# One wait fewer for GpSimd ahead of the cast loads of queries, values and keys

## The chip, the cores and the metric

The kernel runs on one core of one Trainium2 chip. The metric is the device time of one execution in microseconds. The kernel before takes 425.17 us (median of four runs, 424.15 to 426.18).

## The reference

Eight batches of eight heads, with 1152 positions of 64 numbers each, go through attention with pooled queries; the result goes through a feed-forward network without a nonlinearity.

```python
q_pool = q.reshape(B, H, S // 2, 2, D).mean(axis=3)      # 576 queries
scores = scale * q_pool @ k^T                            # 576 x 1152 per head
attn   = softmax(scores)
x      = (attn @ v) as [B*576, 8*64]                     # 4608 x 512
h      = (x @ w1) * (x @ w2) @ w3
out    = h @ w_out                                       # 4608 x 512
```

All inputs and the output are float32 in DRAM. w1 and w2 are 512 x 1024, w3 is 1024 x 1024, w_out is 1024 x 512.

## The kernel before

**Tiling.** Two heads make a pair; there are 32 pairs, four to a batch. For a pair the scores are computed transposed (keys on partitions), key block by key block, and cut into chunks of 512 columns per head. A chunk is computed on TensorE (`scores`, L254), goes through exp on ScalarE (`expo`, L264) into a ring in SBUF, and is multiplied with the values and a column of constants on TensorE (`attend`, L279); VectorE divides by the sums (`normalize`, L292 and L296). The results of two pairs are turned by three DMA transposes on SP's queue into xT (L304, L307), the feed-forward network's input.

**Feed-forward.** The product of w3 and w_out is made once (T). Each unit of 512 tokens then takes the groups pa and pb (x times w1 and w2, L372), gT (their product, on VectorE) and pp (gT times T, L390). An output tile of 128 tokens is written by VectorE in two halves from pp into `osb`, of which there are three buffers (L402), and stored by two DMAs on SP's queue (L411). These groups are fitted in between the attention's work on TensorE; what is left after the attention makes the tail.

**Order.** The order of every engine is written out by hand: one loop over `it`, with three chunks an iteration, and a table (PVS) of how many value products each iteration issues. Each engine runs its own instructions in order, and so does each DMA-issuing queue: SP's and GpSimd's (POOL's) are the two that matter here. The semaphore waits between engines follow from the tiles that are written and read.

**Preparation of queries and keys.** Inputs are loaded by POOL with DMAs that cast to fp16 on the way: `load_q` (L80), `load_k` (L88), `load_v` (L95). For the first eight pairs queries and keys are brought into shape on VectorE and TensorE. From pair 8 on, two pairs at a time go through `prep_dma`: POOL adds neighbouring queries (L121, `pool_q`), POOL copies the keys of each pair into order (L141), and SP issues one DMA transpose of both pairs' keys into kT (L144) and one of both pairs' queries into qT (L147). The loop calls it about two pairs ahead of the scores that need them:

```python
        elif prepped < NP and at >= prepped - 1.95:
            prep_dma(prepped)
            if loaded < NP:
                settled(prepped)
                load_two(loaded)
                loaded += 2
            prepped += 2
```

`settled` lets POOL copy one number out of the kT and one out of the qT just issued (L152), so that POOL stands until the transposes have landed. `load_two` then issues six DMAs on POOL's queue, two each for queries, values and keys of the next two pairs. POOL's next instructions are the additions and copies of that next `prep_dma`, which wait for these loads. This goes round eleven times with loads, for pairs 8 to 28; the last call, for pairs 30 and 31, has none behind it. Of the tiles concerned, kst and vst have four buffers (one a pair), qst, kT, qT and qp two (one for two pairs), kc one.

Of the kernel before, what the change touches and what calls it, by code (L numbers as in the profile page):

```python
# [8 lines left out]
FP16 = mybir.dt.float16  # L9
# [14 lines left out]
def kernel(  # L24
# [11 lines left out]
    nc = tc.nc  # L36
# [12 lines left out]
    const = ctx.enter_context(tc.tile_pool(name="const", bufs=1))  # L49
# [12 lines left out]
    vts = [const.tile([128, 2, NJ, VW], FP16, name=f"vt{i}") for i in range(4)]  # L62

    ident = const.tile([128, 128], FP16)
    seen = const.tile([1, 2], FP16)

    ctx.enter_context(tc.manual_schedule())

# [4 lines left out]
    kst, vst, qst, kT, qT, kTs, qTs, qps = {}, {}, {}, {}, {}, {}, {}, {}  # L73
# [74 lines left out]
            out=qTs[P // 2], in_=qps[P // 2].rearrange("p c u d -> p (c u d)"))  # L148

    def settled(P):  # L150
        for n, t in enumerate((kT[P], qT[P])):
            nc.gpsimd.tensor_copy(out=seen[:, n:n + 1], in_=t[0:1, 0, 0:1])  # L152

    kcs, kc2 = {}, {}

# [207 lines left out]
    def ffn_groups(t):  # L363
# [71 lines left out]
        out=ident, in_=ident, compare_op=ALU.not_equal, fill=1.0,  # L435
# [54 lines left out]
    for c in range(NF):  # L490
        t = (6, 7, 8, 9, 11, 12, 14, 15)[c]
# [14 lines left out]
    for it in range(NIT):  # L506
# [30 lines left out]
        if prepped < NPE:  # L537
            if it >= first_it(prepped) - (1 if prepped < 4 else 2):
                queue[0:0] = prep_groups(prepped)
                prepped += 1  # L540
                urgent = True
# [7 lines that stand above are left out]
# [3 lines left out]
        n = PVS[it]  # L552
# [54 lines left out]
```

## Time and profile before

| what | value |
|---|---|
| median of the runs | 425.17 us |
| profiled execution, own time | 426.18 us |
| its span, first to last instruction | 424.4 us |
| TensorE matmul (PE) busy | 405.2 us, 95% |
| ScalarE (ACT) busy | 326.3 us, 77% |
| VectorE (DVE) busy | 196.5 us, 46% |
| GpSimd (POOL) busy | 123.0 us, 29% |
| granted TensorE clock | 1.0 in all slices |
| loads of q, v, k: issue to landing, median | 5.9, 9.1, 10.7 us |
| kT and qT transposes: issue to landing, median | 4.7, 3.8 us |

The profile comes from the execution of 426.18 us. Its span is 1.8 us shorter than that time, which also has what lies before the first and after the last instruction. A busy TensorE is not a TensorE at its peak: matmuls are pipelined and their ends are modelled. In the table of waits each line says which engine's instruction waited for what, the total in us, how often, and the longest wait. In the chain and in the timelines the first number is the start in us from the beginning of the span and the second is the duration in us; the bracket at the end is the idle time of the engine before it and what ended it. SPq is SyncE's queue, which only issues DMAs. DMA share is the mean busy share of the core's 16 DMA engines; it can pass 1 where packets of several queues overlap on one engine.

### The profile page before, as it was taken

The numbers are of one execution on the slowest core, as the hardware profiler recorded it, in microseconds if no ns is written. First come the engines' busy times: TensorE is split into PE (matmuls) and PEld (weight loads), VectorE is DVE, ScalarE is ACT, GpSimd is POOL, SyncE is SP. The second block draws the span as 40 slices with busy tenths as digits, with TensorE's granted clock in tenths as the row PEclk, the third lists the DMA queues.
The fourth block names the chain that finished last, engine by engine and source line by source line (L and its number), as shares of the span: only waits on it lengthen the run. The fifth ranks groups of instructions, "written<-read, shape, count | busy, mean of one in ns | idle before, by whom it ended". The sixth has DMA issues, their size and how long they took to land.

```text
span 424.4 us, 12581 instructions
## 1 busy us (share of the span) xinstructions
PE 405.2 (95%) x5432; PEld 269.1 (63%) x5432; DVE 196.5 (46%) x406; ACT 326.3 (77%) x355; POOL 123.0 (29%) x171
## 2 busy tenths in 40 slices
PE   3998999999999999999999998999999999999995
PEld 1676777666686577565765685666765876544443
DVE  1446556454544553554454543554445444614130
ACT  4899899989888888988888897887788889133332
POOL 8334321343434215151615243433334000000000
PEclk9999999999999999999999999999999999999999
DMA  8999999598989979698989798988989750050404
GB/s 130 203 208 195 186 192 185 102 167 133 149 144 180 170 112 198 135 188 120 169 149 166 126 146 163 176 146 131 200 151 181 111 117 17 14 116 0 101 0 100
DMA packets 94728, 59.15 MB, mean 139 GB/s; under 512 B 65360, under 2 KB 85072, under 8 KB 94672
## 3 DMA queue, kind: packets, MB, share of 16 engines
q0 software_dynamic: 26544, 33.56, 49.6%
q1 hardware_dynamic: 67968, 24.66, 32.0%
q8 instruction: 42, 0.69, 0.6%
q10 hardware_dynamic: 160, 0.13, 0.1%
q14 instruction: 14, 0.11, 0.1%
HBM read 67.11 MB, written 9.44 MB: 180 GB/s over the span
## 4 chain that ended last, share of the span: by engine, by line
PE 38%; DMA 36%; POOL 10%; SPq 6%; ACT 5%; issue 3%; DVE 1%; POOLq 0%; ACTq 0%; DVEq 0%
DMA kst<-in_k_dram 24%; DMA qT<-qp 8%; PE psc L254 7%; PE po L279 7%; PE pa L372 7%; PE pb L372 7%; PE pp L390 6%; SPq L144 6%; ACT er L264 5%; PE pT L356 3%; POOL vst L95 3%; POOL qst L80 3%; DMA out_dram<-osb 2%; POOL kc L141 2%; POOL kst L88 1%
## 5 line engine op out<-in xcount | busy, mean ns | idle before, releaser
L264 ACT ACTIVATE er<-psc 128x1024 f16<-128x1024 f32 x324 | 307.7, 1025 | 47.1 <-PE psc L254 46.9
L279 PEld LDWEIGHTS <-er 128*128 128x128 f16 x2880 | 104.3, 98 | 23.2 <-issue 6.5
L279 PE MATMUL po<-vt,er 128*128 128x65 f16 x2880 | 111.6, 194 | 0.4 <-DVE xn L296 0.4
L254 PE MATMUL psc<-qT,kT 64*128 64x512 f16 (+7 forms) x1152 | 97.6, 290 | 7.7 <-ACT er L264 3.3
L384 DVE TENSOR_TENSOR gT<-pb,asb 128x512 f16<-128x512 f32 x72 | 49.8, 692 | 55.8 <-PE pb L372 55.1
L372 PE MATMUL pa<-xT,w1sb 128*128 128x512 f16 x288 | 74.2, 380 | 0.0
L372 PE MATMUL pb<-xT,w2sb 128*128 128x512 f16 x288 | 74.1, 380 | 0.0
L390 PE MATMUL pp<-T,gT 128*128 128x256 f16 (+1 forms) x488 | 67.9, 292 | 0.0
L254 PEld LDWEIGHTS <-kT 64*128 64x128 f16 x1152 | 46.5, 95 | 33.3 <-issue 13.5
L382 DVE COPY asb<-pa 128x512 f32<-128x512 f32 x56 | 38.7, 692 | 40.4 <-PE pa L372 39.2
L390 PEld LDWEIGHTS <-gT 128*128 128x128 f16 x488 | 45.6, 98 | 18.5 <-issue 3.7
L372 PEld LDWEIGHTS <-w2sb 128*128 128x128 f16 x288 | 26.4, 98 | 32.7 <-issue 3.9
L372 PEld LDWEIGHTS <-w1sb 128*128 128x128 f16 x288 | 25.1, 98 | 30.1 <-issue 6.2
L121 POOL TENSOR_TENSOR qp<-qst 128x1152 f16<-128x1152 f16 x12 | 28.3, 2357 | 45.5 <-DMA qst<-in_q_dram 45.5
L402 DVE TENSOR_SCALAR osb<-pp 128x256 f32<-128x256 f32 x49 | 20.7, 425 | 41.4 <-PE pp L390 29.7
L292 DVE RECIPROCAL rz<-po 128x5 f32<-128x5 f32 x64 | 12.4, 194 | 49.8 <-PE po L279 49.3
L296 DVE TENSOR_TENSOR xn<-po,rz 128x320 f16<-128x320 f32 x64 | 31.5, 492 | 2.2
L141 POOL COPY kc<-kst 128x576 int32<-128x576 int32 x24 | 16.2, 678 | 45.4 <-DMA kst<-in_k_dram 45.4
L88 POOL DMA_DIRECT2D kst<-in_k_dram x33 | 23.8, 723 | 9.4 <-DMA kst<-in_k_dram 3.8
L95 POOL DMA_DIRECT2D vst<-in_v_dram x32 | 23.2, 727 | 10.6 <-DVE vt L134 5.5
L399 ACT ACTIVATE osb<-pp 128x512 f32<-128x512 f32 (+1 forms) x12 | 7.0, 579 | 24.2 <-PE pp L390 24.2
L80 POOL DMA_DIRECT2D qst<-in_q_dram x32 | 19.9, 622 | 12.0 <-issue 2.7
(40 smaller groups left out, 129.0 us busy)
## 6 DMA issues: line engine op xcount, KB each, us to landing
qst<-in_q_dram POOLq DMA_DIRECT2D x32, 288.0 KB, 5.9
vst<-in_v_dram POOLq DMA_DIRECT2D x32, 288.0 KB, 9.1
out_dram<-osb SPq DMA_DIRECT2D x70, 128.0 KB, 2.4
kst<-in_k_dram POOLq DMA_DIRECT2D x31, 288.0 KB, 10.7
w3h<-in_moe_w_dram POOLq DMA_DIRECT2D x4, 512.0 KB, 14.9
xT<-in_moe_w_out_dram POOLq DMA_DIRECT2D x2, 512.0 KB, 13.9
w1sb<-in_moe_w_dram POOLq DMA_DIRECT2D x2, 512.0 KB, 16.4
w2sb<-in_moe_w_dram POOLq DMA_DIRECT2D x2, 512.0 KB, 17.5
```

The source lines that it names most:

```text
L80: nc.gpsimd.dma_start(out=qst[P // 2][o:o + 64].rearrange("p u t d -> p u (t d)"), in_=q[b, h0:h0 + 2].rearrange("u (p t) d -> p u (t d)", ...
L88: nc.gpsimd.dma_start(out=kst[P][:, :, js[0]:js[1], :], in_=k[b, h0:h0 + 2].rearrange("u (p j) d -> p u j d", j=NJ)[:, :, js[0]:js[1], :])
L95: nc.gpsimd.dma_start(out=vst[P].rearrange("p u j d -> p u (j d)"), in_=v[b, h0:h0 + 2].rearrange("u (p j) d -> p u (j d)", j=NJ))
L121: eng.tensor_tensor(out=qps[pp][r].rearrange("p c u d -> p u c d"), in0=src[:, :, :, 0, :], in1=src[:, :, :, 1, :], op=ALU.add)
L254: nc.tensor.matmul(t[:, u, o:o + ln].rearrange("p (c f) -> p c f", f=64), kT[P][s, j, :], qT[P][s, f0 // 64:(f0 + ln) // 64], start=True, ...
L264: nc.scalar.activation(out=er[:, :, r:r + CH], in_=psc.pop(c), func=AF.Exp, bias=0.0, scale=SCALE)
L279: nc.tensor.matmul(po[P, u][:, VW * x:VW * x + D + 1], er[:, u, r:r + 128], vts[P % 4][:, u, j, 0:D + 1], start=(m == 0), stop=(m == 44), ...
L296: nc.vector.tensor_tensor(out=xn[:, P % 2, :, u, :], in0=acc[:, :, 0:D], in1=rz.to_broadcast([128, 5, D]), op=ALU.mult)
L372: nc.tensor.matmul(p, w[:, mc, ft * 128:ft * 128 + 128], xT[:, mc, t0:t0 + 512], start=(mc == 0), stop=(mc == NC - 1))
L382: nc.vector.tensor_copy(out=asb[ft], in_=p)
L384: nc.vector.tensor_mul(out=gT[:, ft, :], in0=p, in1=asb.pop(ft))
L390: nc.tensor.matmul(p[:, 0:n], gT[:, ft, 128 * i:128 * i + 128], T16[:, ft, n * s:n * s + n], start=(ft == 0), stop=(ft == NF - 1))
```

## The change

`settled` keeps the copy out of kT and drops the copy out of qT; the tile that receives the number shrinks to one element. POOL then issues the six loads after the key transposes have landed, whatever the query transposes do.

```diff
-    seen = const.tile([1, 2], FP16)
+    seen = const.tile([1, 1], FP16)
...
     def settled(P):
-        for n, t in enumerate((kT[P], qT[P])):
-            nc.gpsimd.tensor_copy(out=seen[:, n:n + 1], in_=t[0:1, 0, 0:1])
+        nc.gpsimd.tensor_copy(out=seen, in_=kT[P][0:1, 0, 0:1])
```

## The prediction

> **What bounds the kernel now.** I read the page first (engine rows and the chain that ended last), then the chain in order of time, the table of waits between 80 and 345 us, and the places where TensorE itself stood still.
>
> ```profile
> span 424.4 us, 12581 instructions
> PE 405.2 (95%) x5432; PEld 269.1 (63%) x5432; DVE 196.5 (46%) x406; ACT 326.3 (77%) x355; POOL 123.0 (29%) x171
> PE 38%; DMA 36%; POOL 10%; SPq 6%; ACT 5%; issue 3%; DVE 1%; POOLq 0%; ACTq 0%; DVEq 0%
> ```
>
> TensorE is busy for 95% of the span, yet the chain puts 52% on DMA, POOL and SP. The chain in order of time shows why: from 82 to 294 us it runs round a loop that no compute engine paces. One turn of it:
>
> ```profile
> 270.15 1.24 POOL qst L80 x2
> 271.39 1.43 POOL vst L95 x2
> 273.52 11.85 DMA kst<-in_k_dram
> 286.12 2.70 SPq L144
> 288.86 4.42 DMA qT<-qp
> 294.07 0.89 PE pp L390 x8
> ```
>
> POOL issues six cast loads; the last keys land after 11.85 us; POOL copies them (L141), SP issues the key and the query transposes (L144, L147), and the two copies of line 152 hold POOL until both have landed. Then the next six loads are issued. Turns start at 103.93, 125.89, 150.23 ... 330.26 us by the issues of L144, 22.6 us each on average ((330.26 - 103.93) / 10). TensorE needs two pairs in about the same time: its first score matmuls of pairs 10 and 30 are at 112.8 and 340.3 us, 22.7 us per two pairs. So two things run at almost the same pace, and the question is what the slower one costs the other. The waits answer it:
>
> ```profile
> POOL seen L152 <- DMA kT<-kc: 61.0, 11, 6.6
> POOL seen L152 <- DMA qT<-qp: 11.2, 11, 1.7
> DVE osb L402 <- DMA out_dram<-osb: 4.5, 3, 2.4
> PE psc L254 <- DVE osb L402: 1.9, 2, 1.6
> PE psc L254 <- DMA qT<-qp: 1.2, 2, 0.7
> ```
>
> POOL waits long, but POOL is not the bound. TensorE loses 1.2 us to query transposes (two waits) and 1.9 us to output evictions that wait for an old store (two waits). That 3.1 us is nearly all of its idle time between 80 and 345 us. The places:
>
> ```profile
> 293.32 0.34 PE L254 MATMUL psc<-qT,kT 64*128 64x384 f16 x2 [0.70 <-DMA qT<-qp]
> 257.15 0.40 PE L254 MATMUL psc<-qT,kT 64*128 64x320 f16 x4 [1.64 <-DVE osb L402]
> ```
>
> **The change, part by part.** (1) *The wait and its copy go.* Eleven times POOL no longer waits for qT (11.2 us in all) nor runs the second copy (11 x 0.18 us): 13.2 us, or 1.2 us a turn. One turn, in POOL's timeline:
>
> ```profile
> 268.35 0.18 POOL L152 COPY seen<-kT 1x1 f16<-1x1 f16 x1 [4.83 <-DMA kT<-kc]
> ...
> 269.69 0.18 POOL L152 COPY seen<-qT 1x1 f16<-1x1 f16 x1 [1.16 <-DMA qT<-qp]
> 270.15 1.24 POOL L80 DMA_DIRECT2D qst<-in_q_dram  x2 [0.28 <-issue]
> ```
>
> The first load is issued 0.46 us after the copy that it follows, so it would be issued at 268.81 instead of 270.15.
>
> (2) *What moves.* All six DMAs (two q, two v, two k) move earlier on POOL's queue by that 1.2 us, past the landing of the query transposes and towards what SP issues behind these: the xT transposes (L304, L307) and the output stores (L411). Nothing is reordered on SP. Their buffers are no brake: POOL's loads show no wait for a buffer after 80 us.
>
> Does it hurt the query transposes, which TensorE waits for? Loads and transposes share the 16 DMA engines. The three stretches around the loads of 249.08 us (columns after the engines: granted clock, DMA share, GB/s):
>
> ```profile
> 248.60:249.60 1.00, 1.00 (x14) 0.60 (x14) 0.30 (x1) 0.69 (x2) 0.83 (x2) 1.00 0.38 84
> 249.60:250.30 0.70, 0.70 (x9) 0.63 (x7) 0.00 (x0) 0.70 (x2) 0.70 (x2) 1.00 0.12 22
> 250.30:251.30 1.00, 1.00 (x17) 0.91 (x15) 0.44 (x2) 1.00 (x2) 1.00 (x3) 1.00 0.94 58
> ```
>
> The DMA engines are nearly empty for 1.2 us after the issue: a load moves its first bytes some 1.2 us late. So in the new order the first bytes move about 0.6 + 1.2 = 1.8 us after kT has landed, while qT lands 0.8 to 1.9 us after kT in these eleven turns. The rule that speaks against the change is in the Trainium skill, "DMA: Bandwidth & Descriptors", section "Queues, rings and completion order": each DMA engine goes round-robin, packet by packet, between the queues that have work. By it, a query transpose that met the loads would run at half its pace. By the row the overlap is at most 0.1 us in one turn, so the price on qT is 0.1 us by the rule and nothing by the row; I take nothing. The same rule does bear on what follows qT. In the turns where four or six stores follow (L411 at 267.74, for one), the DMA share is 0.94 between 269 and 272 us: no gap is there to fill, and loads started earlier only share. In the turns where xT transposes follow, the share falls to 0.12 as above, and the 0.9 us saved there is real. So a turn gains between 0 (all shared) and 1.2 us (nothing shared); I take 0.7, nearer the row with the gap, since a load that shares still gets its half.
>
> (3) *What that is worth.* Before pair 18 five turns have been shortened, before pair 26 nine: leads of 5 x 0.7 = 3.5 and 9 x 0.7 = 6.3 us, against waits of 0.49 and 0.70 us. Both go: **-1.2 us**. Less than 0.15 us a turn would do. The lead can grow: the key transposes of pair 18 were issued at 195.2, and the scores that free their buffer ended at 179.0; such a margin is 12 to 16 us in all turns.
>
> (4) *The stores.* SP is in order, and before every turn it stands up to 12 us at L144 waiting for the key copy; stores and xT transposes queue behind. The first output tile of one unit was written at 247.66 but its store was issued at 249.54, behind L307, and landed at 256.55, 6.4 to 7.0 us later because the loads run then (2.4 us when they don't: 269.61 to 272.04). TensorE stood 1.64 us for its buffer. The next unit: written 291.70, issued 295.11, landed 302.62, stall 0.27. With leads of 5 and 6 us SP reaches these stores before they are written: 1.9 and 3.4 us earlier, more than either stall: -1.9 us. Against it: the store of 204.44 (landed 211.42, awaited by DVE for 0.77 us with no stall on TensorE) will fall into the middle of the loads rather than their start, where stores took 6.5 to 7.5 us instead of 5.8 to 6.5; and TensorE comes 0.5 us sooner. I price that at +0.7 us (bounds: 0, if the cover of about 0.8 us at the other stall is there too, and +1.9, if nothing is won on stores at all).
>
> Sum: -1.2 - 1.9 + 0.7 = **-2.4 us**. The profiled execution took 426.18 us (span 424.4 and 1.8 around it); it would take 423.8. It stands 1.0 us above the median of the runs shown, so from 425.17 the forecast is **422.8 us**, 0.6% faster. Everything after 345 us is TensorE's own work and only moves.
>
> **The rivals.** *A, the forecast*, 422.8, own range 421.5 to 423.9; chance 0.50. *B, only the query waits go*: stores find other loads to collide with and their 1.9 us remain: 425.2 - 1.2 = 424.0; chance 0.20. For it: stores and loads are not synchronised, and the lead only shifts where they meet. Against: both stalls had a store held up behind SP's wait for the keys. *C, the change does not shorten the turn*: the loop is limited by DMA work, not by its gaps; the keys then land when they did, and the time stays at 425.2; chance 0.12. For it: DMA shares of 0.88 to 1.01 in all turns. Against: a DMA share of 0.04 from 262.6 to 264.4 us, between the last key load and the first transpose, and the 0.12 above: the engines do idle in every turn. *D, slower: the first store of a unit lands too late.* Its place is the ring of three osb buffers: the fourth tile of a unit needs the first one's. In the unit of 247.66 TensorE would not have stood had the store landed 7.3 us after the tile was written (8.9 - 1.6); the unit of 204.18 took 7.2 without a stall, that of 291.70 took 10.9 with 0.27 us of it. So two units are tight. With loads on top of more stores (the longest store of this profile took 8.3 us from its issue) these two stand for the excess over 7.3 us each. It decides against the change when it costs 1.3 us more than all that is won, (1.2 + 1.9 + 1.3) / 2 + 7.3 = 9.5 us from written to landed; at the 10.9 us of the third unit it is 2 x 3.6 - 3.1 = +4.1 us: 429.3; chance 0.18.
>
> **How the numbers follow.** A measurement of this kernel tells about 0.3% (1.3 us) from no change. A is faster throughout (0.50); of B a quarter comes out just beyond 1.3 us (0.05), the rest is the same (0.15); C is the same (0.12); D is slower (0.18). Faster 0.55, same 0.27, slower 0.18. The range takes in A, B and C and the light end of D: 421.3 to 426.2 leaves out about 0.15 above and 0.05 below.
>
> **What would show it.** Right: eleven seen copies, first load issued 0.5 us after each; issues of L144 creep ahead, so that qT lands more and more before the scores of its pair (0.04 us before at pairs 18 and 26 now); no wait of TensorE on qT; stores of first tiles issued at once. Wrong: query transposes taking over 5 us from issue (they meet the loads after all); turns still 22.6 us long; or longer DVE waits on out_dram with TensorE standing behind them, above all in several units.

## The result, and the profile after

The changed kernel takes 424.58 us (median of 43 executions, 421.73 to 433.73) against 425.04 us (64 executions, 422.60 to 430.46): ratio 0.9972, 95% interval 0.9954 to 0.9990, so 0.28% faster. The ratio leaves out executions far above the fastest of their own kernel, among them the nine of the changed kernel beyond 428 us, which is why it stands below the ratio of the two medians. The mean of all executions has hardly moved: 425.30 us against 425.38. A repetition gave 0.9985 (0.9960 to 1.0010), an interval that reaches no change.

By that ratio the gain is half of the forecast, but it is no uniform half. 13 of the 43 executions took at most 422.6 us, where one of 64 did before; 9 took more than 428, where 6 of 64 did (in the repetition 3 of 22, against 2 of 68). The fastest quarter of the executions took at most 422.4 us, where before it took at most 424.3. So the change makes good executions about 2 us faster and, as it seems, adds bad ones.

The profile was taken of an execution of 426.08 us (span 424.3), 1.5 us above the median and as long as the one profiled before (426.18). Page of the changed kernel; its lines behind `settled` have numbers lower by one:

```profile
span 424.3 us, 12560 instructions
PE 404.5 (95%) x5432; PEld 268.2 (63%) x5432; DVE 197.4 (47%) x406; ACT 326.2 (77%) x355; POOL 121.0 (29%) x160
DMA 54%; PE 32%; POOL 6%; issue 3%; ACT 3%; SPq 1%; DVE 1%; POOLq 0%; DVEq 0%
```

The chain still runs round the loop of loads and transposes. Its waits, 80 to 345 us:

```profile
POOL seen L151 <- DMA kT<-kc: 58.1, 11, 6.6
...
DVE osb L401 <- DMA out_dram<-osb: 3.5, 2, 1.8
...
PE psc L253 <- DMA qT<-qp: 1.9, 3, 1.1
PE psc L253 <- DVE osb L401: 1.4, 2, 0.9
```

POOL's wait for qT is gone. TensorE still waits: 1.9 us for qT (1.2 before) and 1.4 us behind old stores (1.9 before), 3.3 us against 3.1. That explains why this execution is no faster; the question is why the loop got no lead in it. Part of the answer is no effect of the change: the loop of this execution issued the keys of pair 8 at 85.11 us (before: 83.62), 1.5 us late before `settled` was first called. The rest came in the next turn. The longest of the three waits for qT is a new one, at pair 10:

```profile
113.82 0.34 PE L253 MATMUL psc<-qT,kT 64*128 64x384 f16 x2 [1.13 <-DMA qT<-qp]
```

One turn earlier POOL and SP did this (timelines of the changed kernel, POOL's two lines and then SP's two):

```profile
89.85 0.18 POOL L151 COPY seen<-kT 1x1 f16<-1x1 f16 x1 [4.76 <-DMA kT<-kc]
90.34 1.24 POOL L80 DMA_DIRECT2D qst<-in_q_dram  x2 [0.31 <-POOL seen L151]
```

```profile
89.32 4.13 SPq L303 DMA_TRANSPOSE xT<-xn  x2
93.51 1.27 SPq L306 DMA_TRANSPOSE xT<-xn  x1
```

The first load is issued 0.49 us after the copy, as forecast, while the three xT transposes are being issued. Before, the first two of them had been issued by 90.42, about when the first load went out (90.32). What came of it is in the DMA columns (share, GB/s) of two windows, the changed kernel first and then the kernel before at the same stage:

```profile
95.00:99.00 4.00, 4.00 (x95) 3.18 (x91) 1.74 (x4) 3.75 (x5) 0.00 (x0) 1.00 1.10 49
```

```profile
94.50:99.00 4.50, 4.50 (x101) 3.52 (x99) 2.07 (x4) 4.26 (x6) 2.06 (x1) 1.00 1.14 179
```

For 4 us the DMA engines are as busy as ever and move 49 GB/s instead of 179. I call this a crawl. No store had been issued yet (the first is at 116.81 us), so only loads and xT transposes were under way. The DMA view of the same two windows tells whose packets these were (queue, packets, MB, share of the 16 engines; q0 has the loads, q1 the transposes), the changed kernel first:

```profile
q0 software_dynamic: 94, 0.19, 107.9%
q1 hardware_dynamic: 34, 0.01, 2.0%
```

```profile
q0 software_dynamic: 657, 0.81, 113.0%
q1 hardware_dynamic: 35, 0.00, 1.1%
```

The crawl is in the loads' own packets: 1.079 x 16 x 4.0 / 94 = 0.73 us each, against 1.130 x 16 x 4.5 / 657 = 0.12 us. They are not just larger ones. 73 of those that started in the window are the 2304-byte packets of query loads, with a median of 0.95 us; over the whole loop such a packet takes 0.19 us. (One queue alone passes a share of 1 here, so a share over 1 needs no second queue.) The last two xT transposes, meanwhile, landed 10.7 and 10.4 us after their issue instead of 4.1 and 7.1. The last keys of that turn landed 13.2 us after their issue (9.5 before), the turn took 22.5 us instead of 20.3, and TensorE came to qT before it was there. From there on the turns are shorter than before, (328.91 - 107.65) / 10 = 22.1 us against 22.6, but that only made up for the start.

### The profile page after: what moved, and what is told of

It is laid out like the page before. It is cut to its first block, busy times and chain, and to the rows that moved or that the text cites. A ratio compares the mean times of both kernels' runs of the same rounds, so it can differ in the third digit from the quotient of the medians.

```text
span 424.3 us, 12560 instructions
## 1 busy us (share of the span) xinstructions
PE 404.5 (95%) x5432; PEld 268.2 (63%) x5432; DVE 197.4 (47%) x406; ACT 326.2 (77%) x355; POOL 121.0 (29%) x160
## 4 chain that ended last, share of the span: by engine, by line
DMA 54%; PE 32%; POOL 6%; issue 3%; ACT 3%; SPq 1%; DVE 1%; POOLq 0%; DVEq 0%
DMA kst<-in_k_dram 26%; DMA qst<-in_q_dram 11%; DMA kT<-kc 10%; PE pp L389 7%; PE pa L371 7%; PE pb L371 7%; PE po L278 5%; PE psc L253 5%; DMA w2sb<-in_moe_w_dram 4%; ACT er L263 2%; POOL kc L141 2%; POOL qst L80 2%; POOL vst L95 1%; DMA qT<-qp 1%; POOL kst L88 1%
## 5 line engine op out<-in xcount | busy, mean ns | idle before, releaser
L88 POOL DMA_DIRECT2D kst<-in_k_dram x33 | 23.7, 722 | 10.4 <-DVE xn L295 5.4
```

The source lines that it names most:

```text
L88: nc.gpsimd.dma_start(out=kst[P][:, :, js[0]:js[1], :], in_=k[b, h0:h0 + 2].rearrange("u (p j) d -> p u j d", j=NJ)[:, :, js[0]:js[1], :])
```

## The experiments

**A second profile of the changed kernel.** No edit.

> The changed kernel once more, for a second profile. Theory L (the loads of a turn start 1.2 us earlier, the loop gets ahead of TensorE, and the stalls on qT and on old stores go; but in some executions the xT transposes of the first turn meet the loads, the DMA engines crawl for some 4 us, and the lead is lost): 422 to 426 us, median about 424; a profile of about 422 shows no wait of TensorE on qT at pairs 10, 18 and 26, one of about 426 shows the crawl (moving under 90 GB/s at a DMA share over 1) near 95 us. Theory N (the change moves nothing but noise): time as before, 425, with about 3 us of stalls in the profile whatever its time.

Measured: 424.55 us (421.81 to 430.83). The profiled execution was a bad one, 430.83 us. It shows no wait of TensorE for qT at all; the loop was ahead. But it has a crawl, from 248 to 253 us (window of this kernel, DMA share 0.92 at 34 GB/s), in a turn whose xT transposes stood right behind qT, and then the longest stall of TensorE of all:

```profile
248.00:253.00 5.00, 5.00 (x85) 3.91 (x83) 1.64 (x4) 4.37 (x5) 0.00 (x0) 1.00 0.92 34
```

```profile
259.76 0.61 PE L253 MATMUL psc<-qT,kT 64*128 64x320 f16 x4 [4.15 <-DVE osb L401]
```

The first output tile of a unit was written at 247.75 and its store issued at once, at 247.78, into the crawl; it landed at 259.16, 11.4 us after the writing. That is rival D, at its place and beyond its 9.5 us, in one unit. Theory N's stalls of 3 us whatever the time are not what this profile shows (5.0 us behind stores alone); the repetition's interval by itself would still allow N.

The stall cost more than its 4.15 us. The granted clock, 1.00 until then, fell to 0.50 at 257.7 us, 2.1 us into the stall, and stayed there until 264.5. The row of the first matmuls after the stall, and four products of one kind in it and just behind it:

```profile
259.76:264.40 4.64, 4.63 (x29) 2.63 (x29) 0.88 (x2) 1.02 (x1) 1.33 (x2) 0.50 0.46 79
```

```profile
261.99 1.91 PE L371 MATMUL pa<-xT,w1sb 128*128 128x512 f16 x4
266.36 1.03 PE L371 MATMUL pa<-xT,w1sb 128*128 128x512 f16 x4
```

Work that took 4.7 us at half the clock would have taken some 2.4 us less, my estimate, so this one late store cost about 6.5 us in all. The bad executions that were not profiled point the same way: the nine of the changed kernel beyond 428 us have a mean granted clock of 0.989 to 0.997, the thirteen up to 422.6 one of 0.997 to 1.000. The stalls of up to 1.64 us in the kernel before left the clock at 1.0. The forecast had no such cost in it.

**A delay in place of the wait.**

```diff
         nc.gpsimd.tensor_copy(out=seen, in_=kT[P][0:1, 0, 0:1])
+        for _ in range(2):
+            nc.gpsimd.memset(idle, 0)
```

> The changed kernel with two memsets of a spare 128x576 tile on POOL, about 1.2 us, where the wait for qT was: the loads start as late as before without waiting for qT. Theory L: as before, 425, with waits of TensorE on qT of about 1.2 us, since only the start of the loads matters. Rival W (the wait itself, through its semaphore or the order it gives, matters): as the changed kernel, 424.5 or less.

Measured: 426.56 us, ratio to before 1.0031 (1.0010 to 1.0052). The loads started 1.27 us behind the copy in every turn (0.46 in the changed kernel, 1.30 to 2.35 in the kernel before). The gain is gone without the wait being back, so W falls: dropping the wait alone doesn't pay, and an early start is what is left to pay. But the time isn't that of before, it is 0.3% worse, which L did not say. Why a fixed delay is worse than the wait that it replaces stays open.

**Four output buffers**, on either kernel:

```diff
-                    osbs[i] = ffp.tile([128, dm], FP32, tag="osb", bufs=3, name="osb")
+                    osbs[i] = ffp.tile([128, dm], FP32, tag="osb", bufs=4, name="osb")
```

> The kernel before with four osb buffers instead of three. My step on the stores: the fourth tile of a unit no longer waits for the store of the first, the 1.9 us of TensorE behind it go: 425.0 - 1.9 = 423.1. Rival S (the stores are covered by something else that waits next, such as qT): 424.5 to 425.

> The changed kernel with four osb buffers. Theory L: both kinds of stall go: 424.5 - 1.4 = 423.1 in median, its best executions unchanged at about 422, since those have no stall left. Rival S: as the changed kernel, 424.5.

Measured: the kernel before with four buffers 423.27 us, ratio 0.9965 (0.9942 to 0.9987); the changed one 422.83 us, ratio 0.9944 (0.9918 to 0.9971), 421.46 to 426.06. The waits for qT that are left, in the kernel before with four buffers and then in the changed one:

```profile
PE psc L254 <- DMA qT<-qp: 1.4, 1, 1.4
```

```profile
PE psc L253 <- DMA qT<-qp: 0.2, 1, 0.2
```

Neither has a wait for an old store. The stores' part, 1.7 us by the medians, is what step 4 had as 1.9. With four buffers the changed kernel has no execution beyond 426.1 in 15, where with three it had 9 of 43 beyond 428, as if its bad executions reached TensorE through that buffer. Its profile adds to this, for it has a crawl as deep as the first one, in the turn of pair 26:

```profile
291.50:295.50 4.00, 4.00 (x60) 3.42 (x58) 1.91 (x5) 3.35 (x4) 0.00 (x0) 1.00 1.27 51
```

Yet that execution took 421.88 us and TensorE has no stall behind it: with a buffer to spare this crawl was harmless. But the kernel before with four buffers still has 3 of 22 beyond 428, so the counts only point.

**The wait for qT left out in some turns only.** On SP, xT transposes follow qT at once in the turns of pairs 8, 10, 14, 18, 22 and 26; in those of 12, 16, 20, 24 and 28 output stores stand between. The second kernel has the two tuples the other way round.

```diff
-        for n, t in enumerate((kT[P], qT[P])):
+        for n, t in enumerate((kT[P],) if P % 4 == 0 and P > NPE else (kT[P], qT[P])):
```

> POOL waits for kT alone in the five turns in which output stores follow the query transposes on SP (pairs 12, 16, 20, 24, 28), and for both in the six in which xT transposes follow at once (8, 10, 14, 18, 22, 26). Theory X (the gain comes from starting loads early, the losses from loads that start onto the xT transposes): the slow tail goes, median 423.5 to 424.2, no stretch of 3 us or more in which the DMA engines are full and move under 95 GB/s. Rival R (such stretches come whatever lies behind qT): as the changed kernel, 424.5, with a tail beyond 428.

> The other half: kT alone in the six turns in which xT transposes follow qT at once, both in the other five. Theory X: the losses without most of the gain: 425 to 426, with a tail beyond 428 and crawls of 3 us or more in the profile. Rival R: half the gain, 424.8.

Measured: kT alone where stores follow 424.49 us, ratio 0.9997 (0.9970 to 1.0023); kT alone where xT transposes follow 423.62 us, ratio 0.9961 (0.9933 to 0.9989). Theory X had it the wrong way round: where stores follow no gain is measured, where xT transposes follow as much as in all turns together. The two intervals overlap, so this is likely and not certain. The bad executions, too, are with the second kernel (3 of 20 beyond 428, none of 14 in the first, few to go by). Rival R has the median of the first kernel but not its missing tail, and misses the second by 1.2 us.

The second kernel's profile is of a good execution, 422.31 us. Its page and its waits show the forecast as it was meant:

```profile
span 420.5 us, 12565 instructions
PE 87%; ACT 6%; DVE 2%; DMA 2%; issue 1%; POOL 0%; SPq 0%; ACTq 0%; DVEq 0%; POOLq 0%
```

```profile
POOL seen L152 <- DMA kT<-kc: 59.0, 11, 6.6
...
POOL seen L152 <- DMA qT<-qp: 6.9, 5, 2.5
```

The chain is TensorE's own. Between 80 and 345 us no wait of TensorE on qT is left and none of VectorE on a store. Its key transposes are issued 0.9 us earlier than before at pair 10, 3.1 at pair 14 and 4.9 at pair 18 (190.37 instead of 195.23). The first 0.9 is not won by the change: at pair 8 it was there already (82.69 instead of 83.62). SP's timeline from pair 18 on:

```profile
190.37 2.67 SPq L144 DMA_TRANSPOSE kT<-kc  x1
193.09 1.36 SPq L147 DMA_TRANSPOSE qT<-qp  x1
194.55 2.54 SPq L304 DMA_TRANSPOSE xT<-xn  x2
197.13 1.54 SPq L307 DMA_TRANSPOSE xT<-xn  x1
203.29 1.11 SPq L411 DMA_DIRECT2D out_dram<-osb  x2
```

Not all of the lead comes from the missing wait. In this profile kT lands in 4.7 to 4.8 us at pairs 14, 18, 22 and 26, where the kernel before took 5.9 to 6.5, and in 5.5 to 6.4 us at pairs 12, 16 and 28, where that took 4.6 to 4.7. These late landings go with queues that the profile calls instruction (q8 and q14). The kernel before, first from issue to landing of the keys of pair 10 and then of pair 24:

```profile
q1 hardware_dynamic: 3228, 0.82, 92.7%
q8 instruction: 1, 0.02, 0.9%
kT<-kc SPq DMA_TRANSPOSE x1, 6.4
```

```profile
q1 hardware_dynamic: 2944, 0.75, 81.6%
kT<-kc SPq DMA_TRANSPOSE x1, 4.7
```

In the twelve profiles in which POOL waits for kT, 75 of the 144 key transposes had no packet of the instruction queues under way later than 1.3 us after their issue, and every one landed in 4.6 to 4.8 us; of the 69 that had one, 65 took 5.1 to 6.6 us. No experiment moved these packets, so this is what goes together and not a shown cause. At up to 1.8 us it is more than the 1.2 us of the wait, and it falls on other turns in other executions.

**Values ahead of queries.**

```diff
-        load_q(P)
-        load_q(P + 1)
         load_v(P)
         load_v(P + 1)
+        load_q(P)
+        load_q(P + 1)
```

> The changed kernel with the two value loads ahead of the two query loads. Theory Q (the crawl is that of query loads, which fill 64 partitions each, meeting the xT transposes): no crawl of 3 us or more, median 423. Theory X without Q (any load that meets them): as the changed kernel, 424.5, tail beyond 428.

Measured: 424.13 us (421.75 to 432.57), ratio 0.9980 (0.9958 to 1.0002); 5 of 22 executions beyond 428. Theory Q fails as a forecast: the median isn't 423, and the bad executions stay with another kind of load in front. What it says of the crawl isn't refuted. The crawls' packets are mostly those of query loads, and the profile of this kernel, of an execution of 424.91 us, has no crawl. So whether its bad executions have one isn't shown.

**No wait at all**: the call of `settled` is taken out.

> Neither wait: the six loads are issued right behind POOL's key copies and run beside kT and qT. Theory X: transposes and loads now overlap wholly, kT lands 8 us or more after its issue (4.7 before), crawls in most turns; the turn is either shortened all the same (the loads no longer wait for 6 us) or not: 424 to 432. If the loop's length alone mattered (theory L without X), the loop would be far ahead of TensorE, with no wait on qT: 423 as with nothing but store stalls left.

Measured: 435.28 us, ratio 1.0228 (1.0181 to 1.0274). In its profile (439.59 us, its longest execution) the first line is the kT transposes' time from issue to landing between 80 and 345 us, the second TensorE's wait at pair 8:

```profile
DMA to landing us min/median/max: 4.9/12.2/17.5
```

```profile
100.92 1.46 PE L253 MATMUL psc<-qT,kT 64*128 64x512 f16 x10 [8.23 <-DMA qT<-qp]
```

The wait for kT is worth its place: with loads running beside kT and qT, kT lands after 12.2 us (median) where it took 4.7. Here, too, the stall of 8.23 us and a second one of 3.81 us were each followed by the clock at 0.50, for 10.2 and 6.8 us. The length of the loop alone does not decide.

**Without the xT transposes** of pairs 4 to 31, on either kernel:

```diff
-        if u == 0 or P % 2 == 0:
+        if u == 0 or P % 2 == 0 or P > 4:
             return
...
-                                 xT[:, mc, t0:t0 + 512],
+                                 xT[:, mc, 0:512],
```

> The changed kernel without the xT transposes of pairs 4 to 31: the feed-forward groups all read the first 512 tokens of xT, so the work of TensorE is the same and the output is not the reference's. Theory X2 (gain and losses both come from what the earlier loads do to the xT transposes and the transposes to them): no crawl of 3 us or more, no execution beyond 426, median 422. Rival S2 (the slow executions come from stores meeting loads): as the changed kernel, 424.5, tail beyond 428.

> The kernel before without the same xT transposes. Theory X2: kT lands in 4.7 us in all turns instead of 6.4 in the odd ones, turns shorten, the waits on qT go without any change to POOL's waits, and the change has nothing left to win: within 0.5 us of the changed kernel without xT. If the wait for qT costs by itself (1.2 us a turn whatever lies behind it): 1.2 us or more slower than that one.

Measured: the changed kernel without them 422.72 us (421.97 to 425.55), the kernel before without them 421.93 us (421.88 to 422.80). Neither computes the reference's output. Neither has a wait of TensorE on qT or on stores, nor an execution beyond 426 us (of 12 and 6). This speaks against S2, for the stores are all there and the bad executions are gone; it doesn't settle it, since the loop also has less to move and its turns are shorter, (314.13 - 103.78) / 10 = 21.0 us in the kernel before without xT, so that it is well ahead of TensorE. The change has nothing left to win, though POOL still waits 12.0 us for qT in all; so that wait costs nothing by itself, only where the loop is late. One expectation failed: without xT transposes kT still took up to 6.5 us in some turns, so its slow landings are not due to them.

**Both together**: kT alone where xT follows, and four buffers.

> kT alone in the odd turns (xT behind qT), both waits in the others, and four osb buffers. If the loads' early start pays in the odd turns alone and the rest of the tail comes through late stores: median 422.2, no execution beyond 427, below the changed kernel with four buffers (422.8). If the two do not add: 422.8 or more.

Measured: 422.73 us (421.59 to 423.67, 7 executions), ratio to before 0.9936 (0.9910 to 0.9961). This and the changed kernel with four buffers (0.9944) are the fastest versions found that compute the reference, faster than both kernels of this case, and not to be told apart.

## Why the prediction was right or wrong

The range held the time and the direction was right; of 2.4 us the median gave 0.5 and the ratio 1.2. There is luck in that. The range of 421.3 to 426.2 would have held the old time as well, and the forecast proper, rival A at 421.5 to 423.9 with half of the chance, missed the median of 424.58.

*The bound* was read correctly: TensorE loses about 3 us to two kinds of stalls, and without them the kernel takes 422. Three different ways of getting the lead or doing without it (kT alone in some turns, four buffers, no xT transposes) end near there.

*Step 1*, the wait of 1.2 us a turn, was right: the first load goes out some 0.46 us behind the copy instead of 1.30 to 2.35. Its 1.2 us a turn is 0.5 in the length of the turns (22.1 us behind pair 10, against 22.6), and 0.3 of that is kT landing sooner (POOL's waits for kT in these ten turns are 53.4 us instead of 56.2), which fell out so in this execution.

*Step 2* was half wrong. The query transposes are not hurt by the earlier loads, as argued from the 1.2 us that a load needs to move its first bytes: qT's median time to landing between 100 and 320 us is 3.5 us (3.8 before). "A turn gains between 0 and 1.2 us, I take 0.7" has its two ends where I saw them, as far as the two kernels with kT alone in half of the turns can tell: nothing where stores follow (0.9997), the gain where xT transposes follow (0.9961). **The step that failed is "loads started earlier only share".** I took sharing to conserve work: from the round-robin rule (the Trainium skill, "DMA: Bandwidth & Descriptors", section "Queues, rings and completion order") and the shares of 0.94 I concluded that a load that meets other transfers gets its part and they get theirs. The rule says whose turn it is, packet by packet; the halves were my own. And I put even this sharing only on turns with stores: where xT transposes follow I counted the gap of 0.12 as free and the meeting with these transposes at nothing. In the profile of the changed kernel they land after 9.9 us in the median (6.1 before). The profiles of the changed kernel and of its repetition each show one turn in which next to nothing moves for 4 to 5 us instead, and without any wait a kT beside loads took 12.2 / 4.7 = 2.6 times as long and not twice. The two turns with a crawl took 2.2 and 3.2 us longer than the same turns before (22.5 instead of 20.3, 25.6 instead of 22.4), which is more than three turns win at the 0.7 us that I took. What makes the loads' packets so slow isn't shown. All three crawls shown above stand in turns in which POOL waited for kT alone and xT transposes followed qT at once, and the kernels without these transposes have none; but the removal also took DMA work away. That the bad executions which were not profiled have crawls isn't shown either: kT alone where xT follows has them (3 of 20), and the profile of a good one has no crawl.

*Step 3*, the waits on qT, -1.2 us: right where the lead comes about (none left in the repetition and in the good execution above), wrong in the profiled one, where the loop began 1.5 us late, the first turn lost 2.2 us more and the waits became 1.9.

*Step 4*, the stores: the size of 1.9 us was right (1.7 by four buffers). The loss that I priced at 0.7, at the unit whose store falls deeper into the loads, is there: that store of the changed kernel landed 8.0 us after its issue (205.05 to 213.07, 7.0 before), and TensorE stood 0.87 us. Stores gave 0.5 us back in that profile instead of 1.2. What the sum lacked altogether is the clock at half behind a long stall, some 2.4 us in the bad execution.

*Rival D* had the right mechanism and place; its chance was for all executions alike, while it happens in some. *Rival B* (424.0) comes nearest to the measured ratio (0.9972 x 425.04 = 423.9; the median of 424.58 is as near to C), and the repetition's profile has its form, no wait for qT with the stalls behind stores left, though these were 5.0 us and not 1.9; as a typical execution it isn't shown: no good execution of the changed kernel was profiled, and the good one with kT alone in some turns has neither kind of stall. *Rival C* falls with the lead in the kernel with kT alone in some turns, which grew from 0.9 us at pair 8 to 7.9 at pair 24.

## What to carry to other kernels

When a hand-written wait keeps two kinds of DMA apart, count what each of the two does to the other before it is loosened, turn by turn: here dropping the wait for queries gained 0.4% where xT transposes follow and nothing measurable where stores follow, and dropping the wait for keys with it cost 2.3%. A loop that gains lead over the engine it feeds pays only up to that engine's stalls, 3 us here (and what the clock loses behind them), so the stalls' own cure (one more output buffer, 0.35% in the kernel before) can be cheaper than the lead. And look at the spread of the executions beside the median: a change that makes the good ones better and adds bad ones looks like a small gain, and in the mean like none.

## What the runs showed of the hardware

DMA engines can be busy and move little: a share of 1.10 at 49 GB/s for 4 us, 0.92 at 34 GB/s for 5 us and 1.27 at 51 GB/s for 4 us, when cast loads had started while DMA transposes of SBUF tiles were in flight. In the first of these the packets of the loads filled the engines, at 0.73 us each where the kernel before had 0.12. The same two queues moved 179 GB/s at a share of 1.14 in the kernel before.

Key transposes that took 4.7 us in the median behind a wait that kept loads away took 12.2 us beside cast loads. Behind that wait they took 4.6 to 4.8 us without, and mostly 5.1 to 6.6 us with, a packet of the instruction queues under way.

A stall of TensorE of 4.15 us was followed by a granted clock of 0.50 that began 2.1 us into the stall and lasted 6.8 us; stalls of up to 1.64 us in the kernel before were not.
